# A new beginning for a planned attention + MLP kernel: the bias of tile 1 first, scaled identities on ScalarE, three warm-up matmuls

## The chip, the cores and the metric

The kernel runs on one core of one Trainium2 chip. The metric is the device time of one execution in microseconds. The kernel before took 198.78 us in the median of three runs (198.94, 198.78 and 197.07). A profile of one further execution is the source of every other number here.

## The reference, cut to what matters

```python
B, H, S, D = 4, 8, 768, 64            # q, k, v in float32
scores = (q @ k.T) / sqrt(D)
keep = (key < 8) | (0 <= query - key < 96)        # 8 global keys, 96 local ones
bias = -slope[h] * distance                       # global, not local: distance 96
a = softmax(where(keep, scores + bias, -1e9))
x = (a @ v) as [B * S, H * D]                     # 3072 x 512
out = square(relu(x @ w_in)) @ w_out              # w_in 512 x 2048, w_out 2048 x 512
```

The output is float32, 3072 x 512.

## The kernel before

**Tiles and stages.** The 3072 rows are 24 tiles of 128 rows, six to a batch; tiles 0, 6, 12 and 18 are the first of their batch. For tile j the attention part loads q, k and v (GpSimd issues these DMAs, which also turn float32 into bf16), transposes q and k (`tr.0.j` and `tr.1.j` on TensorE into a PSUM bank, then the copies `T.0.j` and `T.1.j`; from tile 8 on a transposing DMA `T.j` on SyncE's queue), forms the scores of the tile's own keys and of the tile ahead (`sc.j`, line 621), takes the exponential (`exp`, ScalarE, line 687), multiplies by the table of biases E (`mul`, VectorE, line 712), multiplies by v (`pv.j`, line 774), divides by the row sums (`norm.j`, VectorE, lines 808 and 809) and transposes the result into `xT` (`trx.j` on TensorE and a copy; from tile 8 on a transposing DMA).

For the first three tiles the bias does not come from `mul`. There `bias.j` (line 600) adds it on TensorE ahead of the scores, into the same bank, as a product of a scaled identity `sid[h]` with the distance table `pb` (or `pb0` for tile 0).

Two tiles make a block of the MLP. Block 0 and half of block 1 go through plain products (`s1.blk.step`, line 1140; then `relu` and `sq`). The other blocks use a seven-product scheme: `h.blk.group.p1` to `p7` (line 1019), with sums of x parts (`xs`, line 988), sums of weight parts made once (`isum`, line 942), copies out of PSUM (`u`), additions with the relu (`c`, line 1064) and squares (`q`). The second product uses a seven-product scheme for all blocks: `s2.blk.p1` to `p7` (line 1279), with `sum` of hidden parts, `wsum` of weight parts made once, `part` and `o` out of PSUM, and the stores `st` on SyncE's queue.

**What sets the order.** A string ORDER has one word per operation. Its words are emitted in turn: each engine gets its instructions in the order of the words that belong to it. A digit string behind `:` gives the PSUM banks or buffers, and `@A` or `@V` moves an operation from its default engine to ScalarE or VectorE. The dependencies are turned into semaphore waits. Every engine works through its own list in order; a word's place in ORDER relative to words of other engines is not a time.

**The beginning.** VectorE clears a tile named zero and eight warm-up matmuls of 128x512 run on it (line 393, their result is not used). GpSimd writes an iota into `pbi`. From it VectorE makes the tables `pbt` and `pbw` (lines 396, 399), the identities in float32 and bf16 (402, 403), `pb` (404), `pb0` (406 to 408), and last the eight `sid` tiles (411). ScalarE loads its table of functions, runs one small exponential (390) and makes E from `pb` with eight exponentials (418). Then GpSimd issues all loads of tiles 1 to 5 and of the weights (line 327), one behind the other, in the order of the words `ld` in ORDER. q and k of tile 0 come over SyncE's queue into `plain`, as float32.

Of the kernel before, what the change touches and what calls it, by code (L numbers as in the profile page):

```python
# [62 lines left out]
ld.v.3 mul.3.1:0 pv.2.1 gv.2@A sc.4.0:3047 exp.4.0.1:1 s1.0.1:6 s1.0.1#2 ld.k.5 ld.q.5 exp.4.1.0:2 mul.3.0:4 pv.3.0:45
pv.3.1 exp.4.0.0 tr.1.5:0 T.1.5@A ld.win.2.0 ld.win.2.1 norm.2:1 trx.2:1 tr.0.5:3 gk.4 norm.3:0 trx.3:4 relu.0.1:0
s1.0.2:5 xT.2@A:1 T.0.5 mul.4.0:4 E0.1 gv.3 xT.3@A exp.4.1.1 sc.5.0:3602 exp.5.1.0:2 sq.0.1:0 s1.0.2#2 ld.v.4 s1.0.2#3
s1.0.2#4 s1.1.1:4 exp.5.0.0 pv.4.0:67 ld.win.3.0 mul.4.1:3 pv.4.1 norm.4:0 ld.win.0.1 ld.win.0.0 xs.1.0:0 relu.0.2:0
exp.5.1.1:3 ld.v.5 relu.1.1:4 s1.1.3:1 isum.0.0 s1.0.3:5 trx.4:6 exp.5.0.1 mul.5.1:1 s1.0.3#2 ld.win.5.0 ld.win.7.0
s1.1.2:4 ld.win.6.0 relu.1.3:5 gv.4 s1.0.0:1 s1.0.0#2 gate.11 s1.0.0#3 E0.0 gate.9 mul.5.0:3 sq.1.1:1 xT.4@A:2 sq.1.3
relu.1.2:4 isum.1.0 xs.1.1 relu.0.3:5 sq.0.3 s1.0.5:0 relu.0.5:2 h.2.0.p1:6 u.2.0.1:5 s1.0.0#4 pv.5.0:34 pv.5.1 isum.3.0
s1.0.7:5 ld.win.4.0 relu.0.7:1 h.2.0.p2:0 norm.5:0 s1.0.6:7 sq.0.2 ld.wout.2 gate.14 relu.0.0:3 h.1.1.p1:5 u.1.1.1:0  # L70
sq.0.7 isum.2.0 relu.0.6:6 sq.0.5 sq.0.6 sq.0.0 h.2.1.p1:3 h.1.1.p2:1 trx.5:4 isum.0.1 h.1.1.p5:2 isum.1.1 h.1.1.p6
u.1.1.2:6 isum.3.1 c.1.1.c11:7 s1.0.4:7 ld.wout.0 relu.0.4:3 u.2.1.1:2 xT.5 s1.1.0:4 c.2.0.c11:0 xs.2.0:1 xs.2.1 xs.1.2
xs.2.2 isum.2.1 h.2.0.p6 u.2.0.2:5 ld.wout.1 ld.wout.3 wsum.0.0 h.1.1.p7 h.2.1.p2:7 sq.0.4 h.2.1.p6 h.2.1.p5:0 h.2.0.p7
s2.0.p2.0:1 u.1.1.3:1 h.1.1.p4 ones.6 wsum.2.0 u.2.1.2:3 wsum.1.0 h.2.1.p7 relu.1.0:8 u.2.0.3:9 u.2.1.3:a sum.0.2:0
ld.wout.5 ld.wout.7 c.1.1.c22:b h.1.1.p3 c.2.1.c11:c q.2.1.c11:2 q.1.1.c22 sq.1.0 h.2.0.p4 c.2.0.c21:b s2.0.p1.0:7
h.2.1.p4 gate.10 sum.0.0 ld.wout.6 ld.wout.4 s2.0.p1.1 h.2.0.p5:4 s2.0.p2.1 sq.1.2 part.0.p1:0 c.2.1.c22:2 h.2.1.p3
load.6.1 c.1.1.c21:4 c.1.1.c12:c wsum.0.1 sum.0.1 tr.0.6:6 tr.1.6:2 c.2.1.c21:8 q.1.1.c12 wsum.1.1 s2.0.p6.0 s2.0.p6.1
part.0.p6:1 o.0.p2:6 s2.0.p5.0 s2.0.p5.1 wsum.2.1 c.2.0.c22:a s2.0.p7.0 s2.0.p7.1 T.1.6@A q.1.1.c21 T.0.6@A wsum.3.0
wsum.3.1 load.8.1 sum.1.0:1 h.2.0.p3 c.2.0.c12:4 part.0.p7:0 o.0.p5:9 q.1.1.c11 c.2.1.c12:5 load.7.1 tr.1.7:2 tr.0.7:6
T.1.7@A T.0.7@A sum.0.3 s2.0.p4.0 s2.0.p4.1 o.0.p4 q.2.0.c22 q.2.0.c12 s2.1.p1.0:4 load.10.0 s2.1.p1.1 part.1.p1:0  # L80
sum.1.1 sum.1.2 sc.6.0:706235 exp.6.0.0:4 q.2.1.c22@V sum.1.3 T.8 exp.6.1.0 mul.6.0:2 s2.0.p3.0 s2.0.p3.1 o.0.p3
exp.7.1.0:a s2.1.p6.0 s2.1.p6.1 exp.7.0.0 s2.1.p2.0:0 s2.1.p2.1 mul.7.0:4 load.6.0 pv.6.0:67 part.1.p6:2 s2.1.p7.0
s2.1.p7.1 o.1.p2:3 load.9.1 exp.7.1.1:7 exp.7.0.1 mul.7.1:a gk.7@A q.2.1.c12 part.1.p7:0 q.2.0.c11 pv.6.1 norm.6:0
gate.13 sc.8.0:3512 gk.8@A exp.8.1.1:7 exp.8.1.0:0 sum.2.0:0 sum.2.1 load.7.0 load.8.0 exp.8.0.1 s2.1.p5.0 s2.1.p5.1
s2.1.p4.0 s2.1.p4.1 load.10.1 o.1.p5:5 pv.7.0:67 pv.7.1 norm.7:1 trx.6:5 exp.8.0.0 mul.8.0:a gv.7@A o.1.p4 s2.2.p1.0:1
s2.2.p1.1 s2.1.p3.0 mul.8.1:4 trx.7:4 xT.6@A:2 xT.7@A T.9 sc.9.0:6732 exp.9.1.0:7 s2.1.p3.1 exp.9.0.1:0 part.2.p1@V:0
xs.3.0:1 pv.8.0:45 pv.8.1 exp.9.0.0 xs.3.1 norm.8:1 h.3.1.p1:7 exp.9.1.1 s2.2.p6.0 u.3.1.1:4 h.3.0.p1:3 h.3.1.p2:4
u.3.0.1:a h.3.0.p2:2 gv.8@A h.3.1.p6 h.3.0.p6 load.11.1 T.10 o.1.p3 mul.9.0:2 mul.9.1:c load.9.0 pv.9.0:56 pv.9.1
c.3.0.c11:7 c.3.1.c11:0 xT.8:1 u.3.1.2:1 u.3.0.2:a h.3.0.p5:2 h.3.1.p7 norm.9:0 xs.3.2 h.3.0.p7 gk.9@A sc.10.0:5640
sum.2.2 u.3.0.3@V:4 c.3.0.c22:c u.3.1.3:2 h.3.1.p4 q.2.0.c21 s2.2.p6.1 exp.10.0.0:d gv.9 T.11 load.12.1 exp.10.1.0  # L90
mul.10.0:4 h.3.0.p4 h.3.1.p5:5 c.3.1.c22:b h.3.0.p3 c.3.0.c12:d exp.10.1.1:e s2.2.p2.0:0 part.2.p6:2 s2.2.p7.0
exp.10.0.1 mul.10.1:2 c.3.1.c21:f q.2.1.c21 q.3.1.c22:1 c.3.0.c21:8 gk.10@A h.3.1.p3 c.3.1.c12:a s2.2.p7.1 part.2.p7@V:1
s2.2.p2.1 o.2.p2:1 pv.10.0:67 pv.10.1 norm.10:1 q.3.0.c22 sum.2.3 q.3.0.c11@V q.3.0.c12 sc.11.0:3524 exp.11.1.0:c
s2.2.p5.0 s2.2.p5.1 o.2.p5:d s2.2.p4.0 exp.11.0.0 gate.12 mul.11.0:7 xT.9 xs.4.0:1 exp.11.1.1:2 exp.11.0.1 h.4.0.p1:5
u.4.0.1:4 q.3.0.c21 h.4.1.p1:3 u.4.1.1:c xs.4.1 h.4.0.p2:4 s2.2.p3.0 s2.2.p3.1 gate.16 c.4.0.c11:b mul.11.1:8 h.4.0.p6
h.4.1.p2:2 u.4.0.2@V:4 xs.4.2 gv.10@A h.4.1.p6 T.12 gate.15 load.11.0 pv.11.0:67 xT.10:2 o.2.p3 load.13.1 pv.11.1
norm.11:0 h.4.1.p5:4 st.1.1 q.3.1.c12 sum.3.0:0 q.3.1.c11 u.4.1.2:a h.4.0.p7 u.4.0.3:8 h.4.1.p7 u.4.1.3:0 h.4.0.p5:0
c.4.0.c22:7 s2.3.p1.0:6 c.4.1.c22:5 q.4.0.c22:0 s2.3.p1.1 h.4.1.p4 part.3.p1:2 c.4.1.c21:7 h.4.0.p4 c.4.0.c21:0 sum.3.1
c.4.1.c11:8 h.4.0.p3 c.4.0.c12:2 q.3.1.c21 h.4.1.p3 s2.2.p4.1 o.2.p4 c.4.1.c12:c sum.3.2 q.4.1.c12@V sum.3.3 load.13.0
q.4.1.c22 load.14.0 s2.3.p6.0 s2.3.p6.1 part.3.p6:1 T.13 st.0.0 q.4.0.c21 sc.12.0:105237 gk.13@A exp.12.0.0:5  # L100
s2.3.p2.0:4 xT.11 xs.5.0:1 exp.12.1.0 s2.3.p7.0 s2.3.p2.1 o.3.p2:c load.14.1 T.14 mul.12.0:0 exp.13.0.0:a exp.13.1.0
s2.3.p7.1 load.15.1 load.12.0 T.15 h.5.1.p1:0 s2.3.p5.0 s2.3.p5.1 part.3.p7:2 xs.5.1 s2.3.p4.0 gate.18 s2.3.p4.1
mul.13.0:5 pv.12.0:12 exp.13.0.1:f o.3.p5:4 u.5.1.1@V:a exp.13.1.1 pv.12.1 mul.13.1:6 st.2.0 norm.12:0 s2.3.p3.0
s2.3.p3.1 o.3.p3 q.4.1.c11 xs.5.2 gate.17 h.5.0.p1:7 xT.12:1 q.4.0.c11 o.3.p4 pv.13.0:56 pv.13.1 q.4.0.c12 h.5.1.p6
norm.13:1 q.4.1.c21 u.5.0.1:2 h.5.0.p2:4 c.5.0.c11:6 u.5.1.2@V:7 h.5.0.p6 u.5.0.2:5 sum.4.0:0 sc.14.0:5612 gk.14
h.5.1.p2:4 s2.4.p1.0:3 h.5.1.p7 h.5.0.p7 s2.4.p1.1 c.5.1.c11:2 sum.4.1 sum.4.3 gv.13 exp.14.0.0:f exp.14.1.0 mul.14.0:a
exp.14.1.1:b exp.14.0.1 u.5.0.3:1 u.5.1.3:0 sc.15.0:2465 h.5.0.p5:1 exp.15.1.1:8 part.4.p1:1 sum.4.2 exp.15.0.1 h.5.0.p4
st.3.0 h.5.1.p4 c.5.1.c21:f load.16.1 T.16 s2.4.p6.0 exp.15.1.0:c exp.15.0.0 mul.14.1:e pv.14.0:56 c.5.0.c22:a gk.15@A
s2.4.p6.1 c.5.0.c21:1 pv.14.1 norm.14:0 q.5.0.c22:1 q.5.0.c21 s2.4.p2.0:0 part.4.p6@V:2 h.5.0.p3 c.5.0.c12:e s2.4.p2.1
o.4.p2:a gate.20 mul.15.0:1 sc.16.0:5672 gk.16 exp.16.0.1:b h.5.1.p5:4 exp.16.1.1 q.5.0.c12 c.5.1.c22:5 h.6.0.p1:1  # L110
s2.4.p7.0 s2.4.p7.1 gv.14@A part.4.p7:1 exp.16.1.0:e q.5.1.c21 q.5.0.c11 mul.15.1:c st.2.1 h.6.1.p1:2 u.6.1.1@V:8 xT.13
s2.4.p5.0 xs.6.0:1 h.5.1.p3 s2.4.p5.1 mul.16.1:0 u.6.0.1:f q.5.1.c11 exp.16.0.0 o.4.p5:d xs.6.1 s2.4.p4.0 load.15.0
# [1386 lines left out]
```

## Time and profile before

| what | value |
|---|---|
| time, median of 3 runs | 198.78 us |
| time of the profiled execution | 197.83 us |
| its span, first to last instruction | 195.9 us |
| TensorE busy | 189.2 us, 97% of the span |
| VectorE busy | 175.1 us, 89% |
| ScalarE busy | 160.1 us, 82% |
| GpSimd busy | 75.2 us, 38% |
| granted TensorE clock | 1.000 |

"Busy" counts an instruction from its start to its end. Matmuls that follow one another overlap, so the work in a stretch is read from the distance of their starts and not from their durations. What lies between the span and the time of the profiled execution is 1.93 us.

### The profile page before, as it was taken

The numbers are of one execution on the slowest core, as the hardware profiler recorded it, in microseconds if no ns is written. First come the engines' busy times: TensorE is split into PE (matmuls) and PEld (weight loads), VectorE is DVE, ScalarE is ACT, GpSimd is POOL, SyncE is SP. The second block draws the span as 40 slices with busy tenths as digits, with TensorE's granted clock in tenths as the row PEclk, the third lists the DMA queues.
The fourth block names the chain that finished last, engine by engine and source line by source line (L and its number), as shares of the span: only waits on it lengthen the run. The fifth ranks groups of instructions, "written<-read, shape, count | busy, mean of one in ns | idle before, by whom it ended". The sixth has DMA issues, their size and how long they took to land.

```text
span 195.9 us, 6859 instructions
## 1 busy us (share of the span) xinstructions
PE 189.2 (97%) x2808; PEld 171.4 (87%) x2808; DVE 175.1 (89%) x389; ACT 160.1 (82%) x337; POOL 75.2 (38%) x93
## 2 busy tenths in 40 slices
PE   7988999999999999999999999999998999999993
...
GB/s 125 147 156 164 181 196 205 207 159 146 150 165 144 131 153 166 171 221 192 185 160 149 100 5 133 135 144 229 104 72 213 84 3 35 77 23 88 0 189 189
DMA packets 111713, 26.92 MB, mean 137 GB/s; under 512 B 103234, under 2 KB 108866, under 8 KB 111682
## 3 DMA queue, kind: packets, MB, share of 16 engines
...
## 4 chain that ended last, share of the span: by engine, by line
PE 84%; POOL 7%; DMA 5%; DVE 2%; issue 1%; ACT 0%; POOLq 0%; DVEq 0%
PE bank L1279 36%; PE bank L1019 33%; PE bank L1140 5%; PE bank L621 5%; POOL qk_first L327 4%; PE bank L774 4%; DMA win<-in_moe_w_in_dram 3%; DMA xT<-x 2%; POOL v L327 2%; DVE xs L988 1%; PE bank L531 0%; PE bank L870 0%; POOL win L327 0%; DVE x L809 0%; DVE hs L1088 0%
## 5 line engine op out<-in xcount | busy, mean ns | idle before, releaser
L1279 PEld LDWEIGHTS <-hsum 128*128 128x128 bf16 x384 | 35.6, 98 | 4.1
L1279 PE MATMUL bank<-wsum,hsum 128*128 128x256 bf16 x288 | 37.7, 273 | 0.0
L1086 ACT ACTIVATE hs<-buf 128x512 bf16<-128x512 f32 x55 | 33.8, 642 | 3.3 <-DVE buf L1064 3.2
L687 ACT ACTIVATE buf<-bank 128x512 bf16<-128x512 f32 x64 | 35.4, 620 | 0.7 <-PE bank L621 0.6
L331 POOL DMA_DIRECT2D qk<-in_q_dram x18 | 15.9, 884 | 48.6 <-DMA qkT<-qk 45.2
L450 ACT COPY buf<-bank 128x512 f32<-128x512 f32 (+1 forms) x44 | 24.5, 564 | 11.4 <-PE bank L1279 5.0
L1019 PEld LDWEIGHTS <-qk_first 128*128 128x128 bf16 x504 | 31.0, 98 | 1.9 <-DVE xs L988 0.8
L1019 PEld LDWEIGHTS <-win 128*128 128x128 bf16 x504 | 30.7, 98 | 0.9
L1279 PEld LDWEIGHTS <-hs 128*128 128x128 bf16 x288 | 26.6, 98 | 2.8
L1279 PE MATMUL bank<-wout,hs 128*128 128x256 bf16 x192 | 26.7, 273 | 0.0
L1019 PE MATMUL bank<-xs,qk_first 128*128 128x128 bf16 x336 | 24.8, 219 | 0.6 <-DVE xs L988 0.5
L1019 PE MATMUL bank<-xT,win 128*128 128x128 bf16 x336 | 23.7, 219 | 0.0
L1064 DVE CUSTOM_DVE_ANT_0 buf<-bank,buf 128x512 f32<-128x512 f32 x29 | 19.7, 684 | 0.4 <-PE bank L1019 0.4
L450 ACT COPY part<-bank 128x256 f32<-128x256 f32 x31 | 11.6, 375 | 8.5 <-PE bank L1279 8.2
L809 DVE TENSOR_TENSOR x<-bank,rs 128x512 bf16<-128x512 f32 x24 | 16.6, 692 | 0.8
L331 POOL DMA_DIRECT2D v<-in_v_dram x18 | 16.0, 898 | 2.3 <-PE bank L1019 2.2
L1234 DVE TENSOR_TENSOR hsum<-hs 128x1024 bf16<-128x1024 bf16 (+1 forms) x26 | 16.4, 642 | 0.1
L331 POOL DMA_DIRECT2D qk<-in_k_dram x18 | 16.0, 887 | 0.8 <-DMA wout<-in_moe_w_out_dram 0.8
L919 ACT ACTIVATE buf<-bank 128x512 f32<-128x512 f32 x25 | 15.0, 624 | 0.1
L1354 DVE TENSOR_TENSOR buf<-bank,part 128x256 f32<-128x256 f32 x32 | 13.4, 418 | 1.3 <-PE bank L1279 1.1
L687 ACT ACTIVATE early<-bank 128x512 bf16<-128x512 f32 x24 | 13.6, 609 | 0.3 <-PE bank L621 0.3
L1086 ACT ACTIVATE hs<-early 128x512 bf16<-128x512 f32 x17 | 11.0, 646 | 3.0 <-DVE early L1064 3.0
...
## 6 DMA issues: line engine op xcount, KB each, us to landing
...
wout<-in_moe_w_out_dram POOLq DMA_DIRECT2D x8, 256.0 KB, 10.0
...
```

The lines of the kernel that those rows point to most:

```text
L327: ("ld",) + name, {"LD": t}, lambda e: nc.gpsimd.dma_start(out=dst, in_=src),
L331: nc.gpsimd.dma_start(out=dst, in_=src)
L450: nc.scalar.copy(dst, src)
L687: nc.scalar.activation(out=tiles[tag, j, g][:, odd], in_=tiles.pop(("sc", j, odd, g)).rearrange("p a c -> p (a c)"), func=Act.Exp, scale=s ...
L809: nc.vector.tensor_tensor(out=x.rearrange("p (b a) c -> p b a c", b=2), in0=po[:, :, :, :D], in1=rs.to_broadcast([P, 2, 4, D]), op=Alu.mult,)
L919: nc.scalar.activation(dst, src, Act.Relu)
L1019: nc.tensor.matmul(out=tiles["h", blk, g, bank][:, n], lhsT=left_[:, s, k], rhs=right_[:, k], start=opens and n == 0 and k == 0, stop=k == ...
L1064: nc.vector._custom_dve(TENSOR_ADD_SAT, out=hr, in0=src, in1=tiles.pop(("u", blk, g, i)), s0=float("inf"), s1=0.0,)
L1086: nc.scalar.activation(hs, hr, Act.Square)
L1234: nc.vector.tensor_tensor(out=t[:, i, h], in0=t[:, a, h] if isinstance(a, int) else half_a(blk, *a)[:, h], in1=t[:, b, h] if isinstance(b, ...
L1279: nc.tensor.matmul(out=tiles["acc", blk, bank][:, cols], lhsT=left_[:, s], rhs=right_[:, cols], start=first and s == 0, stop=s == NSTEP - ...
L1354: nc.vector.tensor_tensor(out=o_sb[:, cols], in0=tiles["acc", blk, bank][:, part], in1=tiles["part", blk, other][:, part], op=Alu.add,)
```

## The change

The number of warm-up matmuls falls from eight to three, the eight scaled identities go from VectorE to ScalarE, VectorE makes the float32 identity first and the bf16 one last, `bias.j` no longer depends on the transposes of its tile, and the table ORDER is another one altogether (its first line stands for it):

```diff
 ORDER = """
-tr.0.0:0 T.0.0@A tr.1.0:1 T.1.0@A ld.k.1 tr.1.1:2 bias.1.0:0345 ld.q.1 tr.0.1:1 bias.0.0:67 sc.0.0 T.1.1 ld.q.2 T.0.1@A
+bias.1.0:0123 tr.0.0:4 T.0.0 tr.1.0:5 T.1.0@A bias.0.0:67 ld.q.1 tr.0.1:4 T.0.1@A ld.k.1 tr.1.1:5 ld.k.2 sc.0.0
...
-    NWARM = 8
+    NWARM = 3
...
+    nc.vector.tensor_scalar(ident32, pbi[:, 0, :], 0.0, None, op0=Alu.is_equal)
+    for h in range(H):
+        nc.scalar.activation(sid[h], ident32, Act.Copy, scale=float(slopes[h] / scale))
     nc.vector.scalar_tensor_tensor(
         out=pbt, in0=pbi, scalar=MASK_VAL, in1=pbi, op0=Alu.mult, op1=Alu.min
     )
...
-    nc.vector.tensor_scalar(ident32, pbi[:, 0, :], 0.0, None, op0=Alu.is_equal)
-    nc.vector.tensor_scalar(ident, pbi[:, 0, :], 0.0, None, op0=Alu.is_equal)
     nc.vector.tensor_tensor(out=pb, in0=pbt, in1=pbw, op=Alu.min)
...
-    for h in range(H):
-
-        nc.vector.scalar_tensor_tensor(
-            out=sid[h], in0=ident32, scalar=float(slopes[h] / scale), in1=ident32,
-            op0=Alu.mult, op1=Alu.mult,
-        )
+    nc.vector.tensor_scalar(ident, pbi[:, 0, :], 0.0, None, op0=Alu.is_equal)
...
-                    lambda e, gs=gs, f=emit_bias: f(e, gs), deps=[tr],
+                    lambda e, gs=gs, f=emit_bias: f(e, gs), deps=[],
```

The last line lets the words `bias.j` stand ahead of the transposes of their tile. The diff also sets an attribute `plan.head`, which nothing reads, and moves one assignment for a list of tiles that is empty here; neither emits an instruction.

Where the new table moves instructions, three places show it.

**ScalarE, from its first instruction.** `early` holds the scaled identities, `ident_96` is the float32 identity, `qkT_80` and `qkT_81` are the transposed q and k of tiles 0 and 1. Before:

```order
L390 ACT_TABLE_LOAD
L390 ACTIVATE junk<-early 128x1
L418 ACTIVATE E<-pb 128x256 x8
L450 CAST qkT_80<-bank 128x512 x2
L450 COPY qkT_81<-bank 128x512
```

And now:

```order
L392 ACT_TABLE_LOAD
L392 ACTIVATE junk<-early 128x1
L400 ACTIVATE early<-ident_96 128x128 x8
L416 ACTIVATE E<-pb 128x256 x8
L448 CAST qkT_80<-bank 128x512
L448 COPY qkT_81<-bank 128x512
```

The eight scaled identities now stand ahead of the eight exponentials, and one of the two casts of tile 0 has gone to VectorE. There is no second load of a table.

**GpSimd, its loads from the first one on.** `qk_first` takes q and k of tiles 1 to 5, `v_71` to `v_76` are v of tiles 0 to 5, and `win` is w_in. Before:

```order
L327 DMA qk_first<-in_k_dram 128x8x64
L327 DMA qk_first<-in_q_dram 128x8x64 x2
L327 DMA v_71<-in_v_dram 128x8x64
L327 DMA qk_first<-in_k_dram 128x8x64
L327 DMA qk_first<-in_q_dram 128x8x64
L327 DMA qk_first<-in_k_dram 128x8x64 x2
L327 DMA v_72<-in_v_dram 128x8x64
L327 DMA v_73<-in_v_dram 128x8x64
L327 DMA qk_first<-in_q_dram 128x8x64
L327 DMA win<-in_moe_w_in_dram 128x4x256
L327 DMA v_74<-in_v_dram 128x8x64
```

And now, from the ninth load on, behind eight loads of q and k:

```order
L329 DMA v_71<-in_v_dram 128x8x64
L329 DMA v_72<-in_v_dram 128x8x64
L329 DMA v_73<-in_v_dram 128x8x64
L329 DMA qk_first<-in_q_dram 128x8x64
L329 DMA qk_first<-in_k_dram 128x8x64
L329 DMA v_74<-in_v_dram 128x8x64
L329 DMA win<-in_moe_w_in_dram 128x4x256
L329 DMA win<-in_moe_w_in_dram 128x4x128 x2
```

The first load of w_in has gone from the twelfth place to the fifteenth, and the first load of v from the fourth to the ninth. The two half loads of w_in behind it stand at the places 16 and 17 in both. The loads behind place 17 keep their kinds but for a few that change places with a neighbour.

**VectorE, up to its first wsum.** `hs` is the squared hidden part, `xs` and `isum` (written into `qk_first` and `plain`) feed the seven-product scheme, `early` and `buf` take what comes out of PSUM, `xT` is the transposed x. Before, the rows that end at the first wsum:

```order
L942 TENSOR_TENSOR plain<-win 128x1024
L1064 ISA buf_120<-bank,early 128x512
L452 COPY xT_108<-bank 128x4x128
L1064 ISA early<-bank,buf_118 128x512
L988 TENSOR_TENSOR xs<-xT_108 128x2x256
L988 TENSOR_TENSOR xs<-xT_108,xs 128x256
L988 TENSOR_TENSOR xs<-xT_107,xs 128x256
L988 TENSOR_TENSOR xs<-xT_108,xs 128x256
L942 TENSOR_TENSOR qk_first<-win,qk_first 128x1024
L1199 TENSOR_TENSOR wsum_91<-wout 128x1024
```

And now:

```order
L940 TENSOR_TENSOR qk_first<-win 128x1024
L940 TENSOR_TENSOR qk_first<-qk_first,win 128x1024
L986 TENSOR_TENSOR xs<-xT_108,xs 128x256
L940 TENSOR_TENSOR qk_first<-win,qk_first 128x1024
L940 TENSOR_TENSOR plain<-win 128x1024
L450 COPY buf_117<-bank 128x512
L1062 ISA early<-bank,buf_118 128x512
L1062 ISA early<-bank,buf_117 128x512
L1197 TENSOR_TENSOR wsum_91<-wout 128x1024
```

Ahead of its first wsum VectorE has two `relu`, one `sq` and one `u` that ScalarE had, one more `c` of line 1064 (now 1062), two more copies `T` and one more `xT`; it has lost one copy `gk` and two copies `gv` to ScalarE. TensorE has the same amount of work ahead of that place in both orders.

More of the change, by code (lines that the diff above doesn't have):

```diff
@@ L63 @@
[L63 to L112, printed above, removed]
@@ new lines @@
+exp.4.0.1 T.0.5 norm.2:0 T.1.5 trx.1:2 xT.1 ld.v.3 pv.3.0:67 pv.3.1 trx.2:4 gk.4@A sc.5.0:0153 ld.win.1.0 s1.0.1:2
+norm.3:1 trx.3:6 gv.3@A xT.2@A:1 mul.4.0:3 xT.3 exp.5.0.0:1 exp.5.1.1:6 exp.5.1.0 s1.0.1#2 ld.win.2.0 ld.win.2.1
+s1.0.2:4 s1.0.2#2 ld.v.4 ld.win.3.0 s1.1.1:6 pv.4.0:01 gate.10 mul.4.1:0 pv.4.1 relu.0.1@V:2 gv.4@A xs.1.0:0 xs.1.1
+norm.4:1 exp.5.0.1 s1.1.2:2 s1.0.3:3 relu.1.1@V:0 trx.4:0 sq.0.1:0 xT.4@A:2 s1.0.3#2 ld.v.5 relu.0.3:2 s1.0.2#3 s1.1.3:6
+s1.0.2#4 relu.0.2:3 mul.5.0:4 ld.win.0.0 s1.0.0:3 ld.win.0.1 s1.0.0#2 mul.5.1:5 sq.1.1:1 isum.0.0 isum.1.0 pv.5.0:01
@@ new lines @@
+pv.5.1 ld.win.5.0 s1.0.5:5 s1.0.0#3 s1.0.0#4 relu.1.2:5 h.2.0.p1:2 sq.1.2 sq.0.3@V isum.3.0 relu.0.0:2 norm.5:1
+ld.win.4.0 s1.0.4:4 ld.win.6.0 xs.1.2 isum.2.0 gate.13 u.2.0.1:5 sq.0.2 trx.5:3 xT.5 h.2.0.p2:0 xs.2.0:1 c.2.0.c11:3
+relu.0.4:0 xs.2.1 s1.0.6:1 relu.0.5:4 sq.0.4 relu.0.6:6 ld.win.7.0 s1.0.7:4 relu.0.7:0 sq.0.5 h.2.1.p1:0 gate.14
+h.2.1.p2:1 isum.0.1 isum.1.1 xs.2.2 isum.2.1 h.2.0.p5:5 u.2.1.1:5 isum.3.1 sq.0.0 sq.0.7 h.1.1.p1:4 u.1.1.1@V:4 h.2.0.p6
+u.2.0.2:2 h.2.1.p5:3 c.2.1.c11:1 h.1.1.p2:7 c.1.1.c11:0 relu.1.3:7 h.2.1.p6 sq.0.6 ld.wout.0 ld.wout.2 ld.wout.3
```

150 lines of the change are left out of this document (96 added, 54 removed).

## The prediction

> **What bounds the kernel now.** First the page's busy times and its row of TensorE in 40 slices.
>
> ```profile
> span 195.9 us, 6859 instructions
> ...
> PE 189.2 (97%) x2808; PEld 171.4 (87%) x2808; DVE 175.1 (89%) x389; ACT 160.1 (82%) x337; POOL 75.2 (38%) x93
> ...
> PE   7988999999999999999999999999998999999993
> ```
>
> TensorE is the bound from the fourth slice on (some 20 us), with VectorE not far behind. What a change of the beginning is worth is decided before that, by how far TensorE has come when it is no longer starved. Who starves it is told by the chain that ended last, up to 25 us (start, length, what):
>
> ```profile
> 0.84 0.34 POOL early L388
> ...
> 1.35 2.77 POOL qk_first L327 x3
> ...
> 11.11 0.75 POOL win L327
> 11.87 0.89 POOL v L327
> 12.75 1.62 POOL qk_first L327 x2
> 14.38 6.16 DMA win<-in_moe_w_in_dram
> ...
> 20.58 0.40 PE bank L1140 x4
> 20.98 0.55 PE bank L621 x16
> 21.53 1.65 PE bank L1140 x20
> 23.18 0.49 PE bank L774 x16
> ...
> 25.01 0.22 PE bank L870 x4
> ```
>
> The path does not run through the warm-ups, the identities or the bias. It is GpSimd, issuing one load after the other, until the 16th load (14.38), whose landing at 20.54 lets s1.0.2 begin at 20.58. The table of waits says what is left elsewhere (total, times, longest):
>
> ```profile
> PE bank L774 <- DMA v<-in_v_dram: 0.6, 1, 0.6
> PE bank L531 <- ACT early L687: 0.5, 2, 0.3
> PE bank L1019 <- DVE xs L988: 0.5, 1, 0.5
> ```
>
> Behind 26 us only the 0.5 us on xs is a named wait. So the change can win in the first 20 us, and little later; it can lose anywhere.
>
> **The first microseconds.** Rows of the timeline (start, length from first to last):
>
> ```profile
> 1.19 3.60 PE L393 MATMUL bank<-early 128*128 128x512 bf16 x8 [1.19 <-DVE early L382]
> ...
> 2.03 0.20 ACT L390 ACTIVATE junk<-early 128x1 f32<-128x1 bf16 x1
> ...
> 3.10 0.17 DVE L407 MEMSET pb<- 8x128 bf16 x1
> ...
> 3.32 2.56 ACT L418 ACTIVATE E<-pb 128x256 bf16<-128x256 bf16 x8 [1.08 <-DVE pb L407]
> 3.40 1.69 DVE L411 SCALAR_TENSOR_TENSOR early<-ident 128x128 bf16<-128x128 f32 x8
> ...
> 4.58 1.91 PE L531 MATMUL bank<-ident,plain 128*128 128x128 f32 x8
> ...
> 6.60 1.04 PE L600 MATMUL bank<-pb,early 128*128 128x256 bf16 x8
> ```
>
> Warm-ups stand (4.58 - 1.19) / 8 = 0.42 us apart, so five fewer end them at about 2.5 instead of 4.6: 2.1 us removed. The bias of tile 1 needs pb (ready at some 3.3 before; now one row earlier or later, 2.9 to 3.4) and the sid tiles. ScalarE's price for a sid is not in the trace. Between VectorE's 1.69 / 8 = 0.21 and the exponentials' 2.56 / 8 = 0.32 (of twice the width) I take 0.22: from 2.2, eight end at 4.0 (4.8 by the upper end). Eight bias matmuls took 1.04 at 0.11 apart; at half that rate, 0.21, they run from 3.0 or 3.3 to 4.8 or 5.0. The float32 transposes (1.91) follow to about 6.8, 0.3 later than before; E ends at 6.6 to 7.4 instead of 5.9. But the bias is out of the way by then: 1.04 us that stood at 6.60. At about 8 us TensorE is thus some 0.5 to 0.8 us further.
>
> **Does that reach the 16th load?** Time from issue to landing (min/median/max): q and k issued up to 11 us, the first w_in (11.02), and q and k issued from 12.6 on.
>
> ```profile
> DMA to landing us min/median/max: 4.8/4.8/5.0
> ```
>
> ```profile
> DMA to landing us min/median/max: 6.2/6.2/6.2
> ```
>
> ```profile
> DMA to landing us min/median/max: 6.3/6.4/6.4
> ```
>
> A load of q, k or v costs GpSimd (12.75 - 11.87) = 0.88 us, one of w_in 0.75. In the new order q, k and v stand at places 1 to 14 and the first w_in at 15: issued at 1.35 + 14 x 0.88 = 13.6, landed 6.2 later, at 19.9. Place 16 is again issued at 14.4 and lands at 20.5, since the same seventeen loads stand in front in both. The twelve q and k of tiles 0 to 5 and four v must land one behind the other, and TensorE's work goes with them: q2, the 4th, lands near 8.9, v0 at 13.2, v3, the 14th, near 17.5. At full rate all of TensorE's work ahead of s1.0.1 is 10.7 us: ten transpositions of q and k (0.22, as the row at 25.01), two in float32 at double rate (0.9), bias (2.2), six sc (five of 0.55, one of half), four pv (0.49, the row at 23.18, and one of half) and three trx (0.22). The most that hangs on one load is 1.6 (q2: a transposition, bias.2, sc.2), and the loads pace the rest, so TensorE is through pv.3 and sc.5 at about 19, with 0.9 us to wait for the first w_in. **This wait swallows the gain of the first microseconds**, and would swallow 0.9 us more of loss.
>
> What is left: ahead of s1.0.2 the new order has the same operations and sc.5 besides, 0.55 us by the row at 20.98. From 19.9 TensorE does s1.0.1, trx.3 and the second half of s1.0.1, 1.1 us at the spacing of the L1140 rows, and starts s1.0.2 at 21.0 instead of 20.58. So 0.55 done, 0.4 later: 0.15 won there. The second half of step 2 (place 17, one load later, 21.3) comes in time, and s1.1.1 no longer stands behind both later quarters of s1.0.2. I take **0.3 us faster**; ends: 0.55 if nothing slips, 0 if the chain of copies in front of sc.5 eats the 0.9.
>
> **xs, later.** One stretch of the chain has 0.5 us of waiting:
>
> ```profile
> 141.38 0.49 PE bank L774 x16
> ...
> 143.40 3.60 DMA xT<-x
> ...
> 147.89 1.51 PE bank L1019 x24
> ```
>
> From the end of pv.19 (141.87) to h.9 (147.89) are 6.0 us: norm, transposing DMA, two xs. TensorE had 5.4 us of other work in its order there. In the new order this place has 7.6 us of work, so the wait goes. The shortest such place is now in block 11: from pv.23 to h.11.0.p6 stand eight groups h (0.45) and five s2 (0.44), 5.8 us: a new wait of 0.2 to 0.3. Net 0.3 faster, 0.6 at most.
>
> **VectorE, 20 to 40 us.** Up to the first wsum, at 26.4 us of TensorE work in both orders, VectorE gets two relu, one sq, one u and one c more, three copies T and xT more, two gv less.
>
> ```profile
> L921 DVE TENSOR_SCALAR buf<-bank 128x512 f32<-128x512 f32 x2 | 1.4, 684 | 0.0
> ```
>
> ```profile
> L452 DVE COPY qkT<-bank 128x512 bf16<-128x512 bf16 x7 | 2.9, 419 | 4.9 <-PE bank L531 4.5 <-ACT early L687 0.3
> ```
>
> With 0.68 for five, 0.42 for three and as much for the two that go: 3.4 + 1.3 - 0.8, some 3.8 us more. Its room there (fourth figure, busy of 4.00, with the count behind it; columns: span, PE, PEld, DVE, ACT, POOL):
>
> ```profile
> 20.00:24.00 4.00, 3.93 (x69) 3.42 (x69) 2.91 (x7) 4.00 (x10) 3.42 (x6) 1.00 1.83 180
> 24.00:28.00 4.00, 4.00 (x54) 3.65 (x52) 3.95 (x11) 4.00 (x10) 3.15 (x5) 1.00 1.52 196
> 28.00:32.00 4.00, 4.00 (x66) 3.81 (x64) 3.61 (x9) 3.67 (x7) 2.06 (x4) 1.00 1.33 203
> 32.00:36.00 4.00, 4.00 (x60) 3.82 (x58) 3.97 (x10) 3.89 (x8) 2.12 (x4) 1.00 1.24 205
> 36.00:40.00 4.00, 4.00 (x71) 3.96 (x69) 4.00 (x10) 3.85 (x9) 3.31 (x4) 1.00 1.33 201
> ```
>
> That is 1.6 us free. Both E0 pairs and the copies T move ahead of 17 us, where VectorE waited for TensorE, and take about 2 us with them. I count 0.4 us of stall; ends: a gain of 0.5 (ScalarE is relieved by the same operations, and 0.5 us of waits were its) and a loss of 3.8 (none of it hidden). Queued behind a late isum or relu on VectorE are norm.5 (trx.5 waits for it) and the c of the first products.
>
> **The end.** The last seven s2 groups and their stores are the same words in both orders. The sums of block 11 stand closer to their user: 5 us of VectorE work against 6.1 of TensorE work behind the last h. Zero, at worst 1 us.
>
> **The sum** against the profiled execution, 197.83 us (span 195.9, 1.93 around it): -0.3 - 0.3 + 0.4 = -0.2, so 197.6. The median of the three runs lies 0.95 above that execution, so I say 198.6. Runs of before differ by 1%, and 1% is about what a measurement of this kernel can tell from no change.
>
> **The rivals.**
>
> *VectorE becomes the bound between 20 and 40 us* (slower). For it: 3.8 us more against 1.6 us of room, and every instruction behind is in order. Against it: much of the added work can start early, and the wsum do not hurry (wout is not used before some 37 us). Without a stall the sum is 198.8 - 0.6 = 198.2; it decides from 2.6 us of stall on (200.8), and if nothing hides it is 198.2 + 3.8 = 202.0. Chance 0.18.
>
> *The clock is released late* (slower). The matmuls show it: 0.42 apart for 512 columns at 1.2 us, 0.11 for 256 at 6.6, twice the rate, while the granted clock of the windows stays 1.00. With three warm-ups TensorE stands still from 2.5 to 3.3. If full rate came only at 10 us, some 2.3 us of work from 6.3 on would take 4.6; the waits for loads and the 0.9 us in front of the first w_in take most of it back, 0.5 us stay, 199.1: within 1%. Slower only if the starved stretch up to 20 us never releases it: the 8.5 us of work left at 6.3 take 17 at half rate and end at 23.3 instead of 19.9, so 198.6 + 3.4 = 202.0. Against it: before, TensorE was as starved from 8 to 20 us and its matmuls stayed fast. Chance 0.05.
>
> The Trainium skill ("TensorE: Matmul & The Clock Gate", part 1 on the HAM clock gate) says that the array starts at half rate and is released after about 3.4 us of sustained activity, in a window that runs freely. Here 5.1 us passed between the first matmul and the first fast one. By the page the gap at 2.5 could put the release off by one more window, which would make the sum that of full rate at 10 us, 199.1 by the estimate above; by the rows alone it stays at 198.6.
>
> *The loads land earlier* (faster). The step from 4.8 to 6.2 us comes with the first w_in. If that pause shrinks because w_in now starts later, w_in lands up to 1.4 us earlier, TensorE is ready at 19, and 0.9 more is won; with the xs wait gone and ScalarE's 0.5 the sum is -2.0: 196.8. Against it: three loads behind the first w_in have 6.3 as well, so the backlog belongs to it. Chance 0.08.
>
> **How the numbers follow.** The forecast, 198.6 with its own range 197.1 (all three good ends: -0.55, -0.6 and -0.5) to 200.7 (where the first rival begins), has 0.69; slower by over 1% 0.18 + 0.05 = 0.23; faster by over 1% 0.08; within 1% 0.69. The range 196.7 to 201.6 leaves out a few hundredths below and most of the unhidden cases above.
>
> **What would show it.** In the changed profile: first landing of w_in at 19.9 and a wait of TensorE for it; s1.0.2 at 21.0; no wait on xs near 147 us, one of 0.3 at h.11; VectorE without idle time from 20 to 40 us. A wait of TensorE on VectorE in that stretch, or starts of 128-column matmuls 0.11 apart after 8 us, would make the prediction wrong.

## The result and the profile after

The changed kernel takes **198.94 us** in the median of 20 runs (197.29 to 200.79), the kernel before 197.77 us in the median of 20 beside it (196.85 to 199.08). The ratio is **1.0055, 95% interval 1.0034 to 1.0075**: slower by half a per cent, where 0.1% faster was forecast. The first three runs of before, with the median 198.78, had been 1.0 us above its median over 20.

The profiled execution took 198.68 us, with a span of 196.9 us (before 195.9). From its page, the busy times, TensorE's 40 slices, and the shares of the chain that ended last by engine:

```profile
span 196.9 us, 6843 instructions
...
PE 188.4 (96%) x2803; PEld 170.9 (87%) x2803; DVE 176.2 (89%) x393; ACT 159.5 (81%) x333; POOL 75.2 (38%) x93
...
PE   7977999999989999899999999999999999999993
...
PE 61%; DMA 21%; POOL 10%; DVE 3%; issue 1%; ACT 0%; SPq 0%; DVEq 0%; POOLq 0%; ACTq 0%
```

The same shares for the kernel before:

```profile
PE 84%; POOL 7%; DMA 5%; DVE 2%; issue 1%; ACT 0%; POOLq 0%; DVEq 0%
```

TensorE's slices dip to 8 twice past the beginning, in the 12th (54 to 59 us) and the 17th (79 to 84), where the kernel before has nines. Its share of the chain has fallen from 84 to 61%, and that of the DMAs risen from 5 to 21%. The pieces of it that hold the new transfers (start, length, what):

```profile
30.21 10.01 DMA wout<-in_moe_w_out_dram
...
40.50 6.93 DMA qk<-in_k_dram
...
47.45 7.80 DMA qkT<-qk
...
55.30 0.62 PE bank L619 x16
...
73.67 0.70 DVE hs L1086
...
74.49 0.38 ACT buf L448
...
74.89 0.33 SPq L1374
...
75.33 8.48 DMA qkT<-qk
...
83.85 0.62 PE bank L619 x16
```

From the loads of w_out on every link up to 55 us is a load or a copy by DMA, down to `T.8`, the transposing DMA of q and k of tile 8 (7.80 us from issue to landing); then `sc.8` begins. A second stretch ends with `T.13` at 83.81, behind a store on SyncE's queue (line 1374). That store waited for its data: ahead of it the chain runs through VectorE from 66.67 to 74.37 us and one copy of ScalarE (74.49). The word `sc.12` forms the scores of tiles 12 and 13 together; those of tile 12 begin at 82.80, those of tile 13, which need `T.13`, at 83.85. The table of TensorE's waits (total, times, longest):

```profile
PE bank L619 <- DMA qkT<-qk: 1.2, 2, 0.7
PE bank L868 <- DVE qkT L450: 0.9, 1, 0.9
```

The 1.2 us on `qkT` are new; before has no such row. (The table counts from the end of the last matmul; counted from where the next one would have started at full-rate spacing, the two stops are 0.66 and 0.84 us, and the expectations below use these.) The 0.5 us on xs is gone. These two make 0.7 of the 1.0 us by which the spans differ; the remaining 0.3 are spread over small pieces that I did not assign.

At the head, TensorE and VectorE in the changed kernel (start, length from first to last):

```profile
2.84 1.86 PE L598 MATMUL bank<-pb,early 128*128 128x256 bf16 x8 [0.18 <-ACT early L400]
...
6.09 0.61 PE L598 MATMUL bank<-pb,early 128*128 128x128 bf16 x8
...
7.34 0.40 PE L619 MATMUL bank<-qkT 64*128 64x128 bf16 x8
```

```profile
18.18 0.38 PE L868 MATMUL bank<-ident,x 128*128 128x128 bf16 x4 [0.87 <-DVE qkT L450]
```

```profile
16.07 0.68 DVE L710 TENSOR_TENSOR early<-buf,E 128x1024 bf16<-128x1024 bf16 x1
16.66 0.68 DVE L710 TENSOR_TENSOR buf<-buf,E 128x1024 bf16<-128x1024 bf16 x1
...
17.73 0.40 DVE L450 COPY qkT<-bank 128x512 bf16<-128x512 bf16 x1
```

The first scores begin at 7.34 instead of 8.24. At 17.31 TensorE stops for 0.87 us, not for w_in but for VectorE's copy out of PSUM at 17.73, which stands behind the two `mul` of tile 3 and `gv.2`.

### The profile page after: what moved, and what is told of

Its sections match the earlier page's. It is cut to its first block, busy times and chain, and to the rows that moved or that the text cites. A ratio compares the mean times of both kernels' runs of the same rounds, so it can differ in the third digit from the quotient of the medians.

```text
span 196.9 us, 6843 instructions
## 1 busy us (share of the span) xinstructions
PE 188.4 (96%) x2803; PEld 170.9 (87%) x2803; DVE 176.2 (89%) x393; ACT 159.5 (81%) x333; POOL 75.2 (38%) x93
## 4 chain that ended last, share of the span: by engine, by line
PE 61%; DMA 21%; POOL 10%; DVE 3%; issue 1%; ACT 0%; SPq 0%; DVEq 0%; POOLq 0%; ACTq 0%
PE bank L1277 29%; PE bank L1017 25%; DMA qkT<-qk 8%; DMA wout<-in_moe_w_out_dram 5%; POOL qk_first L329 5%; DMA win<-in_moe_w_in_dram 4%; PE bank L619 4%; PE bank L772 4%; DMA qk<-in_k_dram 4%; POOL win L329 3%; POOL v L329 3%; DVE buf L1062 1%; ACT buf L448 0%; DVE buf L1352 0%; DVE hs L1086 0%
## 5 line engine op out<-in xcount | busy, mean ns | idle before, releaser
L1084 ACT ACTIVATE hs<-buf 128x512 bf16<-128x512 f32 x64 | 39.6, 642 | 5.3 <-DVE buf L919 2.6
L448 ACT COPY buf<-bank 128x512 f32<-128x512 f32 (+1 forms) x52 | 28.9, 569 | 7.7 <-PE bank L1017 3.9
L1017 PEld LDWEIGHTS <-win 128*128 128x128 bf16 x504 | 31.0, 98 | 1.0 <-DMA xT<-x 0.3
L1017 PEld LDWEIGHTS <-qk_first 128*128 128x128 bf16 x504 | 30.8, 98 | 0.6
L1062 DVE CUSTOM_DVE_ANT_0 buf<-bank,buf 128x512 f32<-128x512 f32 x44 | 29.5, 683 | 1.4 <-PE bank L1017 1.0
L1277 PE MATMUL bank<-wout,hs 128*128 128x256 bf16 x192 | 26.0, 273 | 0.0
L1017 PE MATMUL bank<-xT,win 128*128 128x128 bf16 x336 | 24.4, 219 | 0.0
L1017 PE MATMUL bank<-xs,qk_first 128*128 128x128 bf16 x336 | 24.3, 219 | 0.0
L448 ACT COPY part<-bank 128x256 f32<-128x256 f32 x27 | 10.3, 382 | 10.4 <-PE bank L1277 9.8
L917 ACT ACTIVATE buf<-bank 128x512 f32<-128x512 f32 x23 | 13.7, 607 | 1.5 <-PE bank L1138 0.7
L685 ACT ACTIVATE early<-bank 128x512 bf16<-128x512 f32 x24 | 14.3, 616 | 0.2 <-PE bank L619 0.2
L619 PEld LDWEIGHTS <-qkT 64*128 64x128 bf16 x352 | 10.1, 94 | 5.0 <-DMA qkT<-qk 1.6
L1352 DVE TENSOR_TENSOR buf<-bank,part 128x256 f32<-128x256 f32 x27 | 11.3, 420 | 3.1 <-ACT part L448 1.8
```

Source lines behind the costliest of these rows:

```text
L448: nc.scalar.copy(dst, src)
L619: nc.tensor.matmul(out=tiles["sc", j, odd, g][:, at, :], lhsT=left[j - 1][half, pair, :] if kt else qkT[j % NKT][half, 1, pair, :], rhs=qk ...
L685: nc.scalar.activation(out=tiles[tag, j, g][:, odd], in_=tiles.pop(("sc", j, odd, g)).rearrange("p a c -> p (a c)"), func=Act.Exp, scale=s ...
L917: nc.scalar.activation(dst, src, Act.Relu)
L1017: nc.tensor.matmul(out=tiles["h", blk, g, bank][:, n], lhsT=left_[:, s, k], rhs=right_[:, k], start=opens and n == 0 and k == 0, stop=k == ...
L1062: nc.vector._custom_dve(TENSOR_ADD_SAT, out=hr, in0=src, in1=tiles.pop(("u", blk, g, i)), s0=float("inf"), s1=0.0,)
```

## The experiments

Ratios are to the kernel before, with runs of it on the same chip. That of b1 rests on three executions, those of d3, d4 and d1 on four, six and seven, the others on ten or more.

| kernel | median, us | ratio [95% interval] |
|---|---|---|
| the change | 198.94 | 1.0055 [1.0034, 1.0075] |
| a1: store behind `T.13` | 198.07 | 1.0022 [0.9997, 1.0046] |
| a2: tile 8 loaded ahead of v of tile 10 | 199.03 | 1.0051 [1.0017, 1.0086] |
| a3: a1 and a2 | 197.75 | 1.0003 [0.9980, 1.0025] |
| a4: eight warm-ups again | 198.87 | 1.0061 [1.0037, 1.0086] |
| c1: a3, and `T.22` behind `xT.18` | 197.31 | **0.9970 [0.9947, 0.9992]** |
| e2: c1 without a2's edit | 197.69 | 1.0014 [0.9989, 1.0039] |
| b1: before, `T.13` behind `xT.11` | 201.25 | 1.0159 [1.0092, 1.0225] |
| d4: before, `T.13` behind a store | 199.08 | 1.0074 [1.0046, 1.0103] |
| b2: before, tile 8 loaded behind v of tile 10 | 197.37 | 0.9975 [0.9951, 0.9999] |
| b3: before with the new constants | 198.85 | 1.0048 [1.0023, 1.0073] |
| d3: b3 once more | 198.66 | 1.0072 [1.0045, 1.0099] |
| d1: before with three warm-ups | 198.77 | 1.0072 [1.0044, 1.0100] |
| d2: before with `sid` on ScalarE | 196.81 | 0.9971 [0.9951, 0.9991] |
| e1: d2 and b2 | 197.45 | 0.9974 [0.9952, 0.9997] |

### The copy T.13 behind a store: a1, d4, b1

a1 changes the new order at one place; only SyncE's queue moves:

```diff
-q.4.0.c22@V st.2.1 s2.3.p6.0 s2.3.p6.1 part.3.p6:1 T.13 xT.11
+q.4.0.c22@V s2.3.p6.0 s2.3.p6.1 part.3.p6:1 T.13 st.2.1 xT.11
```

> The changed kernel, with one word moved: the store st.2.1 stands behind the transposing DMA T.13 on SyncE's queue, not ahead of it. Theory (the time went into two late transposing DMAs of q and k): in the changed kernel T.13 waited at 75.33 us behind st.2.1, landed at 83.81, and sc.12 stood 0.84 us for it. Now T.13 is issued at about 73.4, right behind xT.10, lands at about 81.5, and the 0.84 us at 83 go; the wait of 0.66 us near 55 stays. Ratio to the kernel before 1.0055 - 0.0043 = about 1.001. Rival (the loss is spread over the new order, VectorE and ScalarE standing behind at many places): the wait at 83 us comes back elsewhere within 20 us, ratio stays at 1.004 or above.

The time fell by 0.33% to 1.0022 (the two ratios have intervals of ±0.2%). In its trace `T.13` is issued at 74.0 and lands in 6.3 us; no wait on `qkT` is left among TensorE's waits. That of `T.8` is missing too, though its loads were not touched: TensorE came to `sc.8` later in this execution. The two rows of the copy:

```profile
L555 SPq DMA_TRANSPOSE qkT<-qk x1: 1347/1347/1347, 74.0 to 74.0; - x1
...
DMA to landing us min/median/max: 6.3/6.3/6.3
```

The gain holds although this execution was otherwise unlucky at its head (1.1 us of waiting for one load of v).

d4 is the mirror, in the kernel before:

```diff
-part.3.p6:1 T.13 st.0.0 q.4.0.c21
+part.3.p6:1 st.0.0 T.13 q.4.0.c21
```

> The kernel before with one word moved: on SyncE's queue the store st.0.0 goes ahead of the transposing DMA T.13, as a store stands ahead of it in the new order. The store was issued at 75.50, 1.5 us behind T.13, so T.13 issues at about 76.1 instead of 73.95. Theory (the loss at 83 us is the place of T.13 on SyncE's queue): it lands at about 83 to 83.6 instead of 80.99, sc.12, which began at 82.49, waits 0.4 to 1.1 us: ratio 1.002 to 1.006. Rival (the landing is set by the loads in front, whatever the queue does): within 0.2%.

It lost 0.74%, a little beyond the expectation's end, and not by the delay expected. SyncE's queue before, and then in d4:

```profile
73.26 0.57 SPq L1376 DMA_DIRECT2D out_dram<-buf  x1
73.95 1.50 SPq L557 DMA_TRANSPOSE qkT<-qk  x1
75.50 0.58 SPq L1376 DMA_DIRECT2D out_dram<-buf  x1
```

```profile
73.56 1.10 SPq L1376 DMA_DIRECT2D out_dram<-buf  x2
74.77 2.64 SPq L557 DMA_TRANSPOSE qkT<-qk  x1
```

The store was ready, so `T.13` left only 0.8 us later, but it took 9.36 us to land instead of 7.0, and the scores waited for it. The chain of d4 and its row of waits:

```profile
74.77 9.36 DMA qkT<-qk
...
84.17 0.62 PE bank L621 x16
```

```profile
PE bank L621 <- DMA qkT<-qk: 1.0, 1, 1.0
```

What the 0.8 us cost is told by the load of v beside it: before, `T.13` (73.95) left ahead of that load and landed 2.0 us ahead of it; in d4 it left 0.75 us behind it and landed 0.36 behind it. GpSimd's load before, and in d4 (first and last issue; time to landing):

```profile
L331 POOL DMA_DIRECT2D v<-in_v_dram x1: 896/896/896, 74.4 to 74.4; - x1
...
DMA to landing us min/median/max: 8.7/8.7/8.7
```

```profile
L331 POOL DMA_DIRECT2D v<-in_v_dram x1: 881/881/881, 74.0 to 74.0; - x1
...
DMA to landing us min/median/max: 9.7/9.7/9.7
```

So this copy and this load landed in the order in which their issue began, across the two queues, and the copy that had passed behind one load landed 3.1 us later (84.1 against 81.0). That order is frequent in these traces but not a rule: in the kernel before, a copy issued at 80.77 landed in 6.7 us, at 87.49, behind two loads of GpSimd issued at 81.52 and 82.39 that landed in 4.9 us each. The rival of d4 had the first half right (the loads in front set the landing) and the conclusion wrong (here the queue decided which loads were in front). The Trainium skill ("DMA: Bandwidth & Descriptors", sections "Queues, rings and completion order" and "Issuing engines are not separate DMA queues") says that DMAs of both engines run on the same 16 DMA engines, each taking packets of its queues by turns, and that a completion lands only after every earlier write of that DMA engine. By turns alone a copy would not stand behind a whole load; the rule on completions fits what the rows of d4 show, but no run separates it from a common backlog.

b1 moves the word further, behind `xT.11` (in the new order it stands ahead of `xT.11`):

```diff
-part.3.p6:1 T.13 st.0.0 q.4.0.c21 sc.12.0:105237 gk.13@A exp.12.0.0:5 s2.3.p2.0:4 xT.11 xs.5.0:1
+part.3.p6:1 st.0.0 q.4.0.c21 sc.12.0:105237 gk.13@A exp.12.0.0:5 s2.3.p2.0:4 xT.11 T.13 xs.5.0:1
```

> The kernel before, with one word moved: the transposing DMA T.13 goes behind xT.11 on SyncE's queue, as late as the new order has it. Theory (the loss at 83 us is SyncE's order): T.13 issues at about 79 us instead of 73.95 and lands at 84 to 86, where sc.12 wants it at 82.5; a wait of 1.8 to 3.5 us appears there and the time rises by as much, less what a wait further on gives back: ratio to the kernel before 1.006 to 1.018. Rival (the copy lands when the loads in front of it are through, and SyncE's order does not matter): within 0.3%.

The ratio is as the theory said, the place is not. The word now stands behind `sc.12` too, so the scores of tile 13 were formed from what its buffer held (q and k of tile 4; this part of the computation is changed), `sc.12` had nothing to wait for, and `T.13` waited for `sc.12` instead. The wait arose later: everything behind `T.13` on SyncE's queue, and GpSimd's loads into the buffers that it frees, came late, until a copy at 94.62 held up TensorE by 1.8 us:

```profile
84.12 3.18 DMA qkT<-qk
...
87.83 0.75 POOL qk L331
...
88.70 5.90 DMA qk<-in_k_dram
...
94.62 5.95 DMA qkT<-qk
...
100.62 0.62 PE bank L621 x16
```

a1 and d4 show that one place on SyncE's queue is worth 0.3 to 0.7%, as much as the whole change; b1's 1.6% has other waits in it.

### The order of loads at tile 8: a2, a3, b2

a2 puts `load.10.0` (v of tile 10) behind `load.8.1` (q and k of tile 8) again, as before had them; a3 joins it to a1.

```diff
-s2.0.p7.0 load.10.0 s2.0.p7.1 part.0.p7:0 load.8.1
+s2.0.p7.0 s2.0.p7.1 part.0.p7:0 load.8.1 load.10.0
```

> The changed kernel, with one word moved: GpSimd issues v of tile 10 behind q and k of tile 8, not ahead. Theory: T.8 could not start before k of tile 8 had landed (47.43), and its landing at 55.25 held sc.8 up by 0.66 us. Now k of tile 8 lands 0.85 us earlier, T.8 is issued at about 46.6 and lands at about 54.4, just in time for sc.8 at 54.6: the wait falls from 0.66 to 0.0 to 0.1. Ratio 1.0055 - 0.003 = about 1.0025. Rival: T.8's 7.8 us are set by the loads that are queued behind one another and not by its issue; then it lands at 55.2 as before and the ratio stays at 1.0055.

> Both moves together. Theory: the two waits are separate and add up, 0.66 + 0.84 = 1.5 us of 197, so the ratio to the kernel before is 1.0055 - 0.0075 = 0.998, a little faster than before. Rival of a spread loss: 1.003 or above.

In a2 the copy `T.8` lands at 52.06 and the wait at 55 us is gone, but the time stays (1.0051): `T.13` still lands late (0.5 us of waiting on `qkT` in its table). a3 comes to 1.0003. b2 goes the other way in the kernel before, and takes `load.8.1` behind `load.7.1` as well:

```diff
-wsum.3.1 load.8.1 sum.1.0:1
+wsum.3.1 sum.1.0:1
...
-load.10.0 s2.1.p1.1
+load.10.0 load.8.1 s2.1.p1.1
```

> The kernel before, with one word moved: GpSimd issues the load of q and k of tile 8 behind v of tile 10, which is the new order's sequence (tiles 6, 7, v of 10, 8). Theory (the loss at 55 us is the place of that load): the load lands about 2.5 us later, T.8 lands at 54.5 to 55.2 where sc.8 wants it at 53.7, TensorE waits 0.8 to 1.5 us there: ratio 1.003 to 1.008. Rival (the order of two loads is of no account): within 0.2%.

It became faster, not slower. Its `T.8` left at 47.16, as late as in the change, but landed in 6.1 us and not in 7.8, just ahead of `sc.8`. So the sequence of loads alone does not make the wait; where its gain of 0.25% comes from I have not found.

### The next landing: c1, e2

a3's profile has a new wait, `PE bank L1017 <- DMA xT<-x: 0.7`, on a copy of x that SyncE issues right behind two copies of q and k (129.00 and 130.55):

```profile
133.85 7.52 DMA xT<-x
...
141.42 0.62 PE bank L1017 x8
```

c1 is a3 with the second of the two, `T.22`, moved behind `xT.18`, where the kernel before has it too:

```diff
-gv.19 T.22
-norm.19:1
+gv.19 norm.19:1
...
-part.7.p1:1
-xT.18:0 h.9.1.p1:6
+part.7.p1:1 xT.18:0 T.22
+h.9.1.p1:6
```

> The changed kernel with both words put back (v of tile 10 behind q and k of tile 8; the store st.2.1 behind T.13) and T.22 moved behind xT.18 on SyncE's queue, where 0.9 us of waiting stood in the last profile. Theory (what a landing swallows shows as a wait, and the waits are all that the change loses): that wait goes, ratio to the kernel before 0.995 to 0.999. Rival (the next fixed landing behind it takes it back): 1.000, with a new wait behind 140 us; T.22, later by one place, is the likeliest.

The copy of x now lands in 5.4 us and the wait is gone:

```profile
L892 SPq DMA_TRANSPOSE xT<-x x1: 1190/1190/1190, 133.5 to 133.5; - x1
...
DMA to landing us min/median/max: 5.4/5.4/5.4
```

At 0.9970 c1 is faster than both kernels, by three words: 0.85% below the change, of which it is otherwise a copy. Its profiled execution also had a luckier head (0.6 us further at 24 us than that of the change), but the ratio rests on 12 runs.

e2 is c1 without the loads' edit:

> The changed kernel with two words moved on SyncE's queue alone (the store st.2.1 behind T.13, T.22 behind xT.18), its order of loads left as it is. If T.8's wait at 55 us costs what the profile shows (0.66 us): 1.000 to 1.002, against 0.997 with the loads mended too, and a wait of sc.8 in the profile. If that wait is swallowed by what comes behind it: 0.996 to 0.998, whether or not the profile shows it.

1.0014 against c1's 0.9970: 0.9 us, no less than the 0.66 us of `T.8`'s wait in the first profile. But e2's own profile shows no such wait, and the pairs that differ by this edit alone gave 0.04% (a2), 0.19% (a1 and a3) and 0.44% (e2 and c1, measured on two chips), with intervals of ±0.2 to 0.35% on each ratio. What `T.8` costs stays open between nothing and 0.4%.

### The warm-ups and the scaled identities: a4, b3, d1, d2, d3, e1

a4 gives the changed kernel its eight warm-ups back (`NWARM = 8`).

> The changed kernel with eight warm-up matmuls again, all else as changed: TensorE starts the bias of tile 1 at 4.6 instead of 2.84 us. Theory (the loads and the copies behind them swallow what the beginning wins): sc.0 begins some 1.5 us later, at about 8.9, and s1.0.1 is at 20.2 to 20.5 all the same; ratio to the kernel before 1.0055 to 1.007. Rival (the beginning is on the path): 1.5 us slower than the changed kernel, ratio about 1.013.

1.0061 against 1.0055, within the intervals: in the new order five warm-ups more or less make no difference that can be seen. In a4's profile `sc.0` begins at 7.92 instead of 7.34, and `s1.0.1` at 20.32 instead of 20.22. b3 puts the new constants alone (three warm-ups, `sid` on ScalarE, float32 identity first) under the old order:

> The kernel before with the constants of the change alone: three warm-up matmuls, scaled identities on ScalarE, float32 identity first; the table ORDER is that of before. Theory (a gain of the first microseconds is taken back by the waits for the loads up to 20 us): 1.000, within 0.2%, with the fifth-to-last warm-up gone but the first w_in product where it was. Rival (saved work is saved time): 0.9 to 2.1 us less, ratio 0.990 to 0.996.

It lost 0.48%, which neither theory had. The next three runs take it apart. d1 has only `NWARM = 3`, d2 only the constants' engines with eight warm-ups, d3 repeats b3.

> The kernel before with one edit: three warm-up matmuls in place of eight. The constants of the change alone measured 0.48% (about 0.95 us) slower in the order of before, which none of the theories so far gave. Theory A (the pause in front of the first transposes lets the matmuls reach full rate later, and the head no longer has room for it): 1.003 to 1.006 here, with the first 128-column matmuls 0.056 us apart only at 7 us or later (6.4 before). Theory B (it is ScalarE: E and the casts of tile 0 stand behind the eight scaled identities): 1.000 here, within 0.2%.

> The kernel before with the scaled identities on ScalarE and the float32 identity first, and with its eight warm-ups: the other half of the constants. Theory A (the warm-ups): 1.000, within 0.2%. Theory B (ScalarE's queue: E later by eight operations of some 0.2 us, the casts of tile 0 behind it): 1.003 to 1.006, with sc.0 0.5 us or more later than before's 8.24.

> The kernel of b3 once more (before, with the constants of the change alone), for a second profile, since the first was of one of its faster executions (197.71 us against a median of 198.85), and for more times. Theory (the 0.48% is real): 1.003 to 1.007, and a wait in this profile that the first did not have. Rival (it was chance): 1.000 to 1.002.

It is the warm-ups: d1 loses 0.72% by itself, d2 gains 0.29%. TensorE in d1:

```profile
1.19 1.46 PE L393 MATMUL bank<-early 128*128 128x512 bf16 x3 [1.19 <-DVE early L382]
4.22 2.14 PE L531 MATMUL bank<-ident,plain 128*128 128x128 f32 x8 [1.57 <-DVE early L411]
...
6.63 1.92 PE L600 MATMUL bank<-pb,early 128*128 128x256 bf16 x8
8.34 0.63 PE L531 MATMUL bank<-ident,qk_first 128*128 128x128 bf16 x4
```

The old order has nothing for TensorE to do between the third warm-up (ending at 2.65) and the first transpose at 4.22 (the wait is put down to VectorE here, in b3 and d3 to the landing of q of tile 0). After that pause matmuls of 256 columns stand (8.34 - 6.63) / 8 = 0.21 us apart, where the kernel before had 0.11, and those of 128 columns 0.107 until 9.5, with 0.055 from 10.0 on. The profile's granted clock reads 1.00 all the while. d3's execution is the same (the eight matmuls of 256 columns last 1.87 us, and half rate ends near 9.8; 199.71 us), b3's was released at about 7.6 (1.38 us for the same eight; 197.71 us). The eight in b3, then in d3:

```profile
6.79 1.38 PE L596 MATMUL bank<-pb,early 128*128 128x256 bf16 x8
```

```profile
6.80 1.87 PE L596 MATMUL bank<-pb,early 128*128 128x256 bf16 x8
```

With eight warm-ups the six profiles of the old order reach full rate between 4.5 and 7.2 us. These kernels have the same matmuls behind the warm-ups, so their starts can be compared one by one: at 24 us d1 is 1.2 us behind the kernel before and d3 1.3, while b3 is level with it; from there on d1 stays 0.7 to 1.3 us behind. So d1's loss is made at the head. From 4.22 to 21.97 us its chain runs through matmuls, ScalarE and VectorE and holds no load whose landing could have swallowed the delay. The Trainium skill ("TensorE: Matmul & The Clock Gate", part 1 on the HAM clock gate) gives a window of 3.4 us that runs freely: from the first matmul behind the pause, 3.4 us passed in b3 and some 5.5 in d1 and d3, one window or about 1.6. The rows agree with a release after one to two windows.

d3's profile has a second loss, of 1.2 us, at 72.7: `T.11` took 9.3 us to land, against 6.9 in the kernel before, with nothing changed near it:

```profile
63.43 9.30 DMA qkT<-qk
...
72.77 0.62 PE bank L617 x16
```

```profile
PE bank L617 <- DMA qkT<-qk: 1.2, 1, 1.2
```

So a late copy of q and k can hold up TensorE under the old table too; a profile that shows one does not by itself blame the order. For `T.13` the times of a1 and a3 do.

In the new order `bias.1` starts 0.2 us behind the last warm-up, and TensorE goes on at half rate until about 6; the seven profiles with that order (a4's with eight warm-ups among them) reach full rate between 4.8 and 7.0 us. That fits a4, which finds nothing.

e1 joins the two small gains, d2's and b2's:

> The kernel before with the two single edits that each measured about 0.3% faster: scaled identities on ScalarE with eight warm-ups (0.9971), and q and k of tile 8 loaded behind v of tile 10 (0.9975). If both gains are real and lie at different places: 0.993 to 0.996. If one is the other's (both end at the same later landing): 0.997. If they were chance: 0.999 to 1.001.

0.9974: they do not add. d2's gain is thus measured, but not located. ScalarE makes a `sid` in 0.20 us there as in the change (eight from 2.14 to 3.73), near the 0.22 forecast.

## Why the prediction was wrong

**The step that failed is the sentence "Behind 26 us only the 0.5 us on xs is a named wait", and the sum built on it.** It took the waits of the kernel before for the list of places that could matter, allowed in words that the change "can lose anywhere", and gave that no term. The new table moves words on SyncE's queue and on GpSimd's from 30 us on. I compared GpSimd's loads up to place 17 only, and SyncE's queue, with `T.j`, `xT` and the stores in one line, not at all. The missing term is the two copies of q and k that land late: 1.2 us of waits in the profile. Mended on SyncE's queue and in the loads they take the ratio from 1.0055 to 1.0003, and a third place of the same kind takes it to 0.9970 (c1). `T.13`'s share is shown by two pairs that differ by its place alone (the change and a1 0.33%, a2 and a3 0.48%); `T.8`'s stays open between nothing and 0.4%. The slack was there to be read before: `T.13` landed at 80.99, and the first score that reads it began at 82.66. The kernel before has a store directly ahead of `T.13` as well, but one that was ready at 73.26; the store in the new order got its data at 74.87.

**The first microseconds.** The places and landings of w_in came out as said: the first is issued at 13.69 and lands at 19.93 (19.9 forecast), the next at 20.65 (20.5). That the load chain swallows the removed warm-ups is right (a4). The gain left was put at 0.3 (the working has numbers for 0.15 of it) and is about 0: counted by starts and full-rate spacing, TensorE has done some 0.1 us less work at 24 us than before (on w_in 24 matmuls of 128 columns and 16 of 256, against 32 and 13; the rest is alike), and `s1.0.1` starts at 20.22, behind the landing. The low end of that term, "the chain of copies in front of sc.5 eats the 0.9", is what happened; the wait stands on VectorE's copy at 17.73.

**xs.** The wait of before is gone, as forecast, and the new wait of 0.2 to 0.3 at h.11 did not come. That the new order removed it is not shown: in the variants with the old order this wait is not fixed either, b3 has 0.9 us of it, e1 0.5, b2 and d2 none in the table. A term taken from one execution of such a wait is uncertain by its whole size.

**VectorE, 20 to 40 us.** It has indeed less room, busy for 19.59 of the 20 us against 18.43, and TensorE never stands still there. Before and after (columns as in the prediction):

```profile
20.00:40.00 20.00, 19.93 (x307) 18.66 (x307) 18.43 (x44) 19.41 (x40) 14.07 (x19) 1.00 1.45 197
```

```profile
20.00:40.00 20.00, 20.00 (x312) 19.07 (x305) 19.59 (x42) 17.63 (x35) 13.81 (x19) 1.00 1.44 196
```

The stall of 0.4 was not there, nor was the rival of 2.6 us and more.

**The other rivals.** The clock was released at about 6 us in the changed kernel, so that rival is false for it; d1 shows that its mechanism is real in the old order, where the pause is 1.6 us long, and dearer than the 0.5 us I gave it: 0.72%, 1.4 us. The loads did not land earlier: 6.2 us for the first w_in, as before.

**The end.** Zero was right as far as the trace tells: from 164 us on no wait of either kernel stands out.

**The base.** Adding 0.95 us for the median of three runs was a mistake of its own: over 20 runs the median of before is 197.77, at its profiled execution. The forecast time, 198.6, lies near the measured 198.94 only because this error and the missing term point the same way.

So the reading that the beginning itself is worth little was right. With the three places mended (c1) the change measures 0.3% faster (0.08 to 0.53%), against 0.1% forecast; that these lie close is in part luck, since the terms of the sum did not come out one by one. What the forecast lacked is the cost of a table that was rewritten behind the beginning too.
